# Top-k attention and a capacity-limited expert layer: all sign products on GpSimd, the pick's table in PSUM, one order for all steps

## The chip, the cores and the metric

The kernel runs on one core of a Trainium2 chip. A core has five engines with instruction queues of their own: TensorE (PE, with its weight loads as PEld), VectorE (DVE), ScalarE (ACT), GpSimd (POOL) and SyncE (SP, which issues DMAs). Each engine takes its instructions in order; where one needs what another engine makes, it waits for a semaphore. The metric is the device time of one execution in microseconds.

## The reference

Eight batches of eight heads, 576 tokens, head size 64, all float32. A score row keeps its 32 largest entries; the rest become zero after the exponential. The result is the input of a mixture of experts with eight experts, of which each keeps at most 80 tokens.

```python
scores = scale * np.matmul(q, k.transpose(0, 1, 3, 2))
kth = np.partition(scores, -top_k, axis=-1)[..., -top_k:-top_k + 1]   # top_k = 32
scores = np.where(scores >= kth, scores, -1000000000.0)
attn = np.exp(scores - np.max(scores, axis=-1, keepdims=True))
attn = attn / (np.sum(attn, axis=-1, keepdims=True) + 1e-09)
x = np.matmul(attn, v)                       # then (B, H, S, D) -> (4608, 512)

logits = x @ w_gate                          # 8 experts; the best one per token
for e in range(E):
    # the tokens of e, at most the 80 with the largest gate weight
    h = np.maximum(x[tok_idx] @ w1[e], 0.0)
    out[tok_idx] = gate_w[tok_idx, None] * (h @ w2[e])
```

## The kernel before

Attention goes over 32 head pairs (`NP`, four per batch). Of each pair, 576 query rows are cut into four full tiles of 128 rows and a tail of 64. A full tile gives two **units**, one per head; in the tail both heads share one unit of 128 rows. So a head pair has nine units (`UPP`) and the whole attention 288 (`NU`). A unit is 128 rows of 576 scores. After attention come the routing and the experts (`finish`).

What a unit goes through:

- `front`, L226 and L233: TensorE makes the scores of both heads into four PSUM banks; one ScalarE instruction copies them, scaled by a tiny power of two, to the SBUF tile `s`.
- `parts`, L241: VectorE takes the eight largest of each of six blocks of 96 columns into `cand`, six instructions.
- `search`: on the 48 candidates MAX8 (L252) and match-replace (L260) give the 24th largest, in `w9`. ScalarE's `sign` (L257) marks which scores lie below it and counts them into `cnt`. The product `y` of scores and signs (L264), for odd units on GpSimd and for even ones on VectorE, leaves the next candidates as the largest, which MAX8 (L266) finds. The **pick** (L269) compares a table `past` of nine possible counts with `cnt`, and so takes the threshold of the unit into `thr`.
- `below`, L278 and L280: the mask of all scores under the threshold, for odd units by ScalarE, for even ones by GpSimd.
- `turn_w`, L316 to L325: TensorE transposes the scores of a tile into `ab` and `cc` and adds the masks times a huge negative number (L321); two ScalarE exponentials give `wT`.
- `back`, L336: `wT` times the values, with a column of ones, into `cc`. `over`, L348: the reciprocal of the sums. `divide`, L359: two ScalarE copies per tile scale the result into the features `xn`.
- `norm`, L368 to L392: the features are stored to DRAM; transposed (`xT`, L376) and multiplied by the gate weights, they give the logits (`part` or `lg`, L388).
- `turn`, L201 and L214: transposes q and k of the next head pair; one ScalarE copy takes both out (`both`).

PSUM has eight banks here: four in the pool `ps_s`, two in `ps_w` (`ab`), two in `ps_c` (`cc`). `four()` takes a new tile of all four banks of `ps_s`, and `turn`, `front`, `norm` (twice) and the last `turn_w` use it in turn. The pool `rows` holds the big SBUF tiles.

`run` writes the order by hand (`manual_schedule`): no planner moves an instruction. In step i each letter of a string places one instruction of a unit that lies `back[c]` steps back, so that several units are in different stages. "G" is one of the six MAX8 of unit i; "a" the last of them and the first MAX8 of the search; "b", "c", "d", "e" the rest of the search of unit i-1, "e" with `sign`; "y" the product of unit i-2; "g" its MAX8 a step later; "h" the pick of unit i-4 and "m" its mask; "z" the reciprocal. After the letters a step places `turn_w` of unit i-4, the `divide`, `front` of unit i+4, `back` of unit i-5, and then `turn` or a part of `norm`.

```python
back = dict(a=0, b=1, c=1, d=1, e=1, y=2, g=3, h=4, m=4)

for c in "ghmGbGycGdGGGeaz" if i % 2 else "GbGhmgcGdGeGGyaz":
```

The weights of experts 0 to 3 load beside attention, in pieces from the list `slow` (L137), expert 4's when `finish` begins, those of 5 to 7 as buffers come free.

Of the kernel before, what the change touches and what calls it, by code (L numbers as in the profile page):

```python
# [18 lines left out]
TOP_K = 32  # L19
# [8 lines left out]
def kernel(  # L28
# [120 lines left out]
    class Attention:  # L149


        def __init__(self, stack, lean):
            self.lean = lean
            pool = lambda name, bufs, **kw: stack.enter_context(tc.tile_pool(name=name, bufs=bufs, **kw))
            self.nat, self.qkp, self.rows = pool("nat", 1), pool("qkp", 2), pool("rows", 2)
            self.small, vpool = pool("small", 4), pool("vpool", 1)
            self.ps_s, self.ps_w, self.ps_c = (pool(n, k, space=PSUM) for n, k in (("ps_s", 1), ("ps_w", 1), ("ps_c", 2)))
            self.qk, self.turned, self.lg = {}, {}, {}
            self.s, self.top, self.cnt, self.y, self.mask, self.w, self.xn = ({} for _ in range(7))
            self.thr, self.z = thr_all, z_all  # L160
# [32 lines left out]

        def four(self):
            return self.ps_s.tile([P, 4, 512], F32, name="sp", tag="sp")

# [6 lines left out]
        def turn(self, n):  # L203

            four = self.four()
            ps = [four[:, 2 * j : 2 * j + 2, :].rearrange("p j c -> p (j c)") for j in range(2)]
            both = self.qkp.tile([P, 2, S], F32, name="both", tag="both")
            self.turned[n] = both[:, 0, :], both[:, 1, :]
            for j, src in enumerate(self.qk.pop(n)):
                self.turn_in(ps[j], src.rearrange("p c h d -> p c (h d)"))  # L210
                if n == 0:
                    nc.scalar.copy(both[:, j, :], ps[j][:, :S])
            if n > 0:
                nc.scalar.copy(both, four.rearrange("p (k j) c -> p k (j c)", k=2)[:, :, :S])  # L214

        def front(self, n, t):

            qT, kT = self.turned[n]
            m = P if t < NF else TL
            i = n * UPP + 2 * t  # L220
            ps = self.four()
            for j in range(2):
                for h in range(2):
                    d = slice(D * h, D * h + D)
                    o = ps[:, 2 * h + j, :HS] if t < NF else ps[TL * h : TL * h + TL, j, :HS]
                    nc.tensor.matmul(o, lhsT=qT[d, t * P : t * P + m], rhs=kT[d, j * HS : (j + 1) * HS], start=True, stop=True)  # L226
            g = 2 if t < NF else 1
            s = self.rows.tile([P, 2 * S], F32, name="s", tag="s", bufs=2 if self.lean else 5)
            for h in range(g):
                self.s[i + h] = s[:, h * S : (h + 1) * S]  # L230
            for j in range(0, 2 * g, 2 if i == 0 else 2 * g):
                w = 2 if i == 0 else 2 * g
                nc.scalar.activation(s[:, j * HS : (j + w) * HS].rearrange("p (j c) -> p j c", c=HS), ps[:, j : j + w, :HS],  # L233
                                     Act.Copy, scale=TINY)
# [10 lines left out]
        def search(self, i):  # L245
# [4 lines left out]
            for r in range(G0 // 8):  # L250
# [8 lines left out]
                if r < G0 // 8 - 1:  # L259
                    nc.vector.match_replace(out=cand, in_to_replace=dst, in_values=cand, imm_value=LOW)  # L260
# [3 lines left out]
            engine.tensor_tensor(out=y, in0=s, in1=sign, op=Alu.mult)  # L264
            yield
            nc.vector.max(out=w9[:, 8:], in_=y)  # L266
            yield
            pick = self.small.tile([P, TOP_K - G0 + 1], F32, name="pick", tag="pick")
            nc.vector.scalar_tensor_tensor(out=pick, in0=past, scalar=cnt, in1=w9[:, 7:], accum_out=self.thr[:, i : i + 1],  # L269
                                           op0=Alu.is_equal, op1=Alu.mult)  # L270
# [11 lines left out]
        def search_all(self, i):  # L282

            s = self.s[i]
            top = self.top[i] = self.small.tile([P, TOP_K // 8, 8], F32, name="top", tag="top")
            scr = self.rows.tile([P, S], F32, name="y", tag="y", bufs=1)
            nc.vector.max(out=top[:, 0, :], in_=s)
# [12 lines left out]
        def turn_w(self, n, t):  # L300
# [3 lines left out]
            if i == NU - 1 and not self.lean:  # L304

                ab = self.four().rearrange("p h (c r) -> p h c r", r=P)
            else:
# [42 lines left out]
        def divide(self, n, t):  # L350
            if t == 0:
                self.xn[n] = self.rows.tile([P, NK, 2, D], F32, name="xn", tag="xn")
            cc = self.w.pop((n, t))
            for h in range(2):
                if t < NF:
                    p, o, j, m = slice(0, P), 2 * P + h * (D + 1), h, P
                else:
                    p, o, j, m = slice(TL * h, TL * h + TL), 2 * P, 0, TL
                nc.scalar.activation(self.xn[n][:m, t, h, :], cc[p, o : o + D], Act.Copy, scale=self.z[p, n % NP, t, j : j + 1])  # L359

        def norm(self, n, b, hp, bi, nb, cs=range(NK)):
# [9 lines left out]
            yield 1  # L371
            ps = self.four()[:, :2, :].rearrange("p j c -> p (j c)")
            at = slice(cs[0] * P, min(S, cs[-1] * P + P))
# [3 lines left out]
            yield 1  # L377
            lp = self.four()[:, 0, : NK * E].rearrange("p (c e) -> p c e", e=E)
            for c in cs:
# [48 lines left out]
        def run(self, slow):  # L428
# [17 lines left out]
            def step(i, last):  # L446
# [424 lines left out]
    with tc.If(nc.values_load(bad[0:1, 0:1]) > 0):  # L871
# [6 lines left out]
        with ExitStack() as again:  # L878
            wpool = again.enter_context(tc.tile_pool(name="wpool2", bufs=4))
            for e in range(4):  # L880
                for dma in load_w(e, wpool):
# [33 lines left out]
```

## Time and profile before

| | |
|---|---|
| median of 3 runs | 996.0 us (993.81 to 996.81) |
| profiled execution: its time / its span | 994.79 us / 993.1 us |
| VectorE busy | 870.6 us (88%), 5072 instructions |
| TensorE busy, weight loads | 885.5 us (89%), 704.9 us |
| ScalarE busy | 797.2 us (80%), 1652 instructions |
| GpSimd busy | 451.9 us (46%), 330 instructions |
| first and last pick | at 20.5 and 859.3 us |
| first expert's first matmul | at 901.2 us |

Busy time is the union of an engine's instructions. VectorE's and ScalarE's overlap by some tens of ns where they follow each other, so that the mean duration of a group is more than what one of them costs; the distance from a start to the next start, in the timeline, is the better price. A group's line gives the count, the busy time and mean duration, and after the second bar the idle time of the engine before these instructions, with who ended most of it.

### The profile page before, as it was taken

What the parts mean: (1) busy time and instruction counts of PE and PEld (TensorE: products, weight loads), DVE (VectorE), ACT (ScalarE), POOL (GpSimd) and SP (SyncE); (2) the same over time, 40 slices, a digit from 0 to 9 for tenths busy, and PEclk for the clock granted to TensorE, in tenths of its full rate; (3) what the DMA queues carried; (4) which work ended last, traced back from release to release, by engine and by line L of the source; (5) the groups of instructions that cost most, each with busy time, mean ns of one, the idle gap of its engine ahead of it and who ended that gap; (6) DMA issues with size and microseconds to landing.
All of it is one profiled execution on the core that took longest, in us unless ns stands there. A gap on an engine that the chain in (4) does not pass through costs nothing.

```text
span 993.1 us, 35590 instructions
## 1 busy us (share of the span) xinstructions
PE 885.5 (89%) x13368; PEld 704.9 (71%) x13368; DVE 870.6 (88%) x5072; ACT 797.2 (80%) x1652; POOL 451.9 (46%) x330
## 2 busy tenths in 40 slices
PE   5899999998989989899899999999899898679996
PEld 3677777776767777677677777777677676668896
DVE  5899999999999999999999999999999999571110
ACT  3899999999999989999999999999899999601110
POOL 2445555555455545554555555555455555302111
PEclk9999999999999999999999999999999999979998
DMA  3344453333332323333333322222222100044920
GB/s 72 97 126 131 129 134 92 92 92 92 91 79 62 87 82 86 92 92 93 88 82 83 91 49 51 50 50 50 50 50 49 41 23 14 16 170 142 382 76 28
DMA packets 167893, 85.76 MB, mean 86 GB/s; under 512 B 117792, under 2 KB 154656, under 8 KB 167712
## 3 DMA queue, kind: packets, MB, share of 16 engines
q1 hardware_dynamic: 166688, 80.78, 29.7%
q0 software_dynamic: 1024, 2.62, 0.9%
q8 instruction: 107, 1.75, 0.7%
q14 instruction: 74, 0.61, 0.2%
HBM read 63.19 MB, written 20.19 MB: 84 GB/s over the span
## 4 chain that ended last, share of the span: by engine, by line
DVE 53%; PE 24%; ACT 18%; issue 5%; DMA 1%; POOL 0%; POOLq 0%; SPq 0%; ACTq 0%; DVEq 0%
DVE cand L241 17%; DVE w L266 12%; DVE cand L260 6%; DVE y L264 6%; ACT s L233 4%; DVE top L252 4%; PE yp L799 4%; ACT wT L325 3%; PE sp L201 3%; PE cc L336 3%; ACT sign L257 3%; DVE pick L269 3%; ACT mask L278 2%; PE sp L226 2%; PE ab L316 2%
## 5 line engine op out<-in xcount | busy, mean ns | idle before, releaser
L241 DVE MAX8 cand<-s 128x8 f32<-128x96 f32 x1728 | 393.9, 250 | 8.9 <-ACT s L233 8.8
L280 POOL TENSOR_SCALAR mask<-s,thr_all 128x576 bf16<-128x576 f32 x144 | 248.2, 1723 | 144.9 <-DVE pick L269 121.8
L264 POOL TENSOR_TENSOR y<-s,sign 128x576 f32<-128x576 f32 x144 | 184.8, 1283 | 277.3 <-DVE pick L269 128.0
L336 PEld LDWEIGHTS cc<-vb,wT 128*64 128x64 f32 x5760 | 181.7, 138 | 111.2 <-ACT wT L325 98.5
L257 ACT ACTIVATE sign<-s,w 128x576 bf16<-128x576 f32 x288 | 225.4, 783 | 22.8 <-DVE w L252 22.2
L336 PE MATMUL cc<-vb,wT 128*64 128x65 f32 x5760 | 204.0, 225 | 40.6 <-ACT wT L325 38.9
L266 DVE MAX8 w<-y 128x8 f32<-128x576 f32 x288 | 217.8, 756 | 2.5 <-POOL y L264 2.5
L226 PE MATMUL sp<-both 64*128 64x288 f32 (+1 forms) x1280 | 202.1, 435 | 15.0 <-ACT part L388 6.5
L233 ACT ACTIVATE s<-sp 128x1152 f32<-128x1152 f32 (+1 forms) x161 | 167.3, 1040 | 12.7 <-PE sp L226 11.9
L316 PE MATMUL ab<-ident,s 128*128 128x128 f32 x1148 | 175.6, 282 | 0.0
L325 ACT ACTIVATE wT<-ab 128x1024 f32<-128x1024 f32 (+1 forms) x159 | 148.8, 936 | 0.0
L226 PEld LDWEIGHTS sp<-both 64*128 64x128 f32 (+1 forms) x1280 | 105.6, 179 | 53.8 <-ACT part L388 8.5
L316 PEld LDWEIGHTS ab<-ident,s 128*128 128x128 f32 x1148 | 127.5, 141 | 11.6 <-issue 0.9
L321 PEld LDWEIGHTS <-mask 128*128 128x128 bf16 x1440 | 92.1, 98 | 42.4 <-ACT mask L278 19.6
L252 DVE MAX8 top<-cand 128x8 f32<-128x48 f32 x576 | 116.9, 203 | 0.0
L260 DVE MATCH_REPLACE8 cand<-top,cand 128x48 f32<-128x48 f32 x576 | 112.9, 196 | 0.0
L278 ACT ACTIVATE mask<-s,thr_all 128x576 bf16<-128x576 f32 x144 | 112.3, 780 | 0.4
L264 DVE TENSOR_TENSOR y<-s,sign 128x576 f32<-128x576 f32 x144 | 107.6, 747 | 4.5 <-ACT sign L257 4.5
L359 ACT ACTIVATE xn<-cc,z_all 128x64 f32<-128x64 f32 (+1 forms) x320 | 86.5, 318 | 1.4 <-DVE z_all L348 0.8
L316 PE MATMUL cc<-ident,s 128*128 128x128 f32 x288 | 78.9, 274 | 0.3 <-ACT xn L359 0.2
L269 DVE SCALAR_TENSOR_TENSOR pick<-past,cnt,w 128x9 f32<-128x9 f32 x288 | 69.5, 241 | 0.2 <-DVE z_all L348 0.2
L323 ACT ACTIVATE wT<-cc 128x256 f32<-128x256 f32 (+1 forms) x160 | 56.2, 351 | 12.0 <-PE cc L321 11.3
(188 smaller groups left out, 965.7 us busy)
## 6 DMA issues: line engine op xcount, KB each, us to landing
w<-in_moe_w_dram SPq DMA_DIRECT2D x32, 512.0 KB, 4.7
w<-in_moe_w_dram SPq DMA_DIRECT2D x8, 2048.0 KB, 9.8
out_dram<-zero SPq DMA_DIRECT2D x9, 1024.0 KB, 6.3
qn<-in_q_dram SPq DMA_DIRECT2D x64, 128.0 KB, 2.6
kn<-in_k_dram SPq DMA_DIRECT2D x64, 128.0 KB, 2.5
vb<-in_v_dram SPq DMA_DIRECT2D x64, 128.0 KB, 2.6
xd<-xn SPq DMA_DIRECT2D x32, 256.0 KB, 4.3
qn<-in_q_dram SPq DMA_DIRECT2D x32, 32.0 KB, 2.5
```

Of the source, the lines that this page charges most:

```text
L226: nc.tensor.matmul(o, lhsT=qT[d, t * P : t * P + m], rhs=kT[d, j * HS : (j + 1) * HS], start=True, stop=True)
L233: nc.scalar.activation(s[:, j * HS : (j + w) * HS].rearrange("p (j c) -> p j c", c=HS), ps[:, j : j + w, :HS], Act.Copy, scale=TINY)
L241: nc.vector.max(out=cand[:, j, :], in_=s[:, j * S // NG : (j + 1) * S // NG])
L252: nc.vector.max(out=dst, in_=cand)
L257: nc.scalar.activation(sign, s, Act.Sign, bias=w9[:, 7:8], scale=-1.0, accum_out=cnt)
L260: nc.vector.match_replace(out=cand, in_to_replace=dst, in_values=cand, imm_value=LOW)
L264: engine.tensor_tensor(out=y, in0=s, in1=sign, op=Alu.mult)
L266: nc.vector.max(out=w9[:, 8:], in_=y)
L280: nc.gpsimd.tensor_scalar(self.mask[i], self.s[i], self.thr[:, i : i + 1], None, op0=Alu.is_lt)
L316: nc.tensor.matmul(dst[h][c], lhsT=sc[:, keys[c]], rhs=ident, start=c == 0 or (c == NF and h == 0), stop=False, is_transpose=True, skip_gr ...
L325: nc.scalar.activation(wT[:, : g * NF, :], ab.rearrange("p h c r -> p (h c) r")[:, : g * NF, :], Act.Exp, scale=scale / TINY)
L336: nc.tensor.matmul(cc[r : r + TL, o], lhsT=wT[:, h * NF + c if c < NF else 2 * NF + h, r : r + TL], rhs=vb[:, c, h if t < NF else r // TL, ...
```

## The change

All 288 products go to GpSimd, and the tile `y` gets two buffers. The features of a full tile are made by one VectorE product out of PSUM, with the reciprocals spread over the columns; the tail's by two. The tile `banks` takes the four PSUM banks once and for all; `four(w, step)` gives views of it, and its last 16 columns hold a copy of the table `past`, which the pick now reads. One string gives the order of all steps, with the pick first and the features ("x") last. To make room for the second `y`, the weight pool has three buffers and the late one two: expert 3's weights load in `finish`.

```diff
-            self.ps_s, self.ps_w, self.ps_c = (pool(n, k, space=PSUM) for n, k in (("ps_s", 1), ("ps_w", 1), ("ps_c", 2)))
+            ps_s, self.ps_w, self.ps_c = (pool(n, k, space=PSUM) for n, k in (("ps_s", 1), ("ps_w", 1), ("ps_c", 2)))
+            self.banks = ps_s.tile([P, 4 * 512], F32, name="banks")
+            self.past = self.banks[:, 4 * 512 - 16 :][:, : TOP_K - G0 + 1]
+            nc.vector.tensor_copy(self.past, past)
...
-        def four(self):
-            return self.ps_s.tile([P, 4, 512], F32, name="sp", tag="sp")
+        def four(self, w, step=512):
+            t = self.banks[:, :]
+            return bass.AP(t.tensor, t.offset, [list(t.ap[0]), [step, 4 * 512 // step], [1, w]])
...
-            y = self.rows.tile([P, S], F32, name="y", tag="y", bufs=1)
-            engine = nc.gpsimd if i in self.odd else nc.vector
-            engine.tensor_tensor(out=y, in0=s, in1=sign, op=Alu.mult)
+            y = self.rows.tile([P, S], F32, name="y", tag="y")
+            nc.gpsimd.tensor_tensor(out=y, in0=s, in1=sign, op=Alu.mult)
...
-            nc.vector.scalar_tensor_tensor(out=pick, in0=past, scalar=cnt, in1=w9[:, 7:], accum_out=self.thr[:, i : i + 1],
+            nc.vector.scalar_tensor_tensor(out=pick, in0=self.past, scalar=cnt, in1=w9[:, 7:], accum_out=self.thr[:, i : i + 1],
...
+            o, xn, z = 2 * P, self.xn[n], self.z[:, n % NP, t, :].unsqueeze(2)
+            if t < NF:
+                nc.vector.tensor_tensor(out=xn[:, t, :, :], in0=cc[:, o : o + 2 * (D + 1)].rearrange("p (h d) -> p h d", h=2)[:, :, :D],
+                                        in1=z.to_broadcast([P, 2, D]), op=Alu.mult)
+                return
             for h in range(2):
...
-                nc.scalar.activation(self.xn[n][:m, t, h, :], cc[p, o : o + D], Act.Copy, scale=self.z[p, n % NP, t, j : j + 1])
+                p = slice(TL * h, TL * h + TL)
+                nc.vector.tensor_tensor(out=xn[:TL, t, h, :], in0=cc[p, o : o + D], in1=z[p, 0, :].to_broadcast([TL, D]), op=Alu.mult)
...
-                for c in "ghmGbGycGdGGGeaz" if i % 2 else "GbGhmgcGdGeGGyaz":
+                for c in "hmybGcGdGeGGGgzax":
...
+                    elif c == "x":
+                        for u in drawn:
+                            self.divide(*u)
...
-                for u in done:
-                    self.divide(*u)
...
-        late = stack.enter_context(tc.tile_pool(name="late", bufs=1))
-        for dma in load_w(4, late):
-            dma()
+        late = stack.enter_context(tc.tile_pool(name="late", bufs=2))
+        for e in (3, 4):
+            for dma in load_w(e, late):
+                dma()
...
-        wpool = main.enter_context(tc.tile_pool(name="wpool", bufs=4))
-        for e in range(4):
+        wpool = main.enter_context(tc.tile_pool(name="wpool", bufs=3))
+        for e in range(3):
             slow += load_w(e, wpool, 4)
```

More of the change, by code (lines that the diff above doesn't have):

```diff
@@ L203, in turn @@
         def turn(self, n):
-            four = self.four()
-            ps = [four[:, 2 * j : 2 * j + 2, :].rearrange("p j c -> p (j c)") for j in range(2)]
+            ps = self.four(S, 1024)
             both = self.qkp.tile([P, 2, S], F32, name="both", tag="both")
@@ L209, in turn @@
             for j, src in enumerate(self.qk.pop(n)):
-                self.turn_in(ps[j], src.rearrange("p c h d -> p c (h d)"))
+                self.turn_in(ps[:, j, :], src.rearrange("p c h d -> p c (h d)"))
                 if n == 0:
-                    nc.scalar.copy(both[:, j, :], ps[j][:, :S])
+                    nc.scalar.copy(both[:, j, :], ps[:, j, :])
             if n > 0:
-                nc.scalar.copy(both, four.rearrange("p (k j) c -> p k (j c)", k=2)[:, :, :S])
+                nc.scalar.copy(both, ps)
         def front(self, n, t):
@@ L220, in front @@
             i = n * UPP + 2 * t
-            ps = self.four()
+            ps = self.four(HS)
             for j in range(2):
@@ L224, in front @@
                     d = slice(D * h, D * h + D)
-                    o = ps[:, 2 * h + j, :HS] if t < NF else ps[TL * h : TL * h + TL, j, :HS]
+                    o = ps[:, 2 * h + j, :] if t < NF else ps[TL * h : TL * h + TL, j, :]
                     nc.tensor.matmul(o, lhsT=qT[d, t * P : t * P + m], rhs=kT[d, j * HS : (j + 1) * HS], start=True, stop=True)
@@ L232, in front @@
                 w = 2 if i == 0 else 2 * g
-                nc.scalar.activation(s[:, j * HS : (j + w) * HS].rearrange("p (j c) -> p j c", c=HS), ps[:, j : j + w, :HS],
+                nc.scalar.activation(s[:, j * HS : (j + w) * HS].rearrange("p (j c) -> p j c", c=HS), ps[:, j : j + w, :],
                                      Act.Copy, scale=TINY)
@@ L285, in search_all @@
             top = self.top[i] = self.small.tile([P, TOP_K // 8, 8], F32, name="top", tag="top")
-            scr = self.rows.tile([P, S], F32, name="y", tag="y", bufs=1)
+            scr = self.rows.tile([P, S], F32, name="y", tag="y")
             nc.vector.max(out=top[:, 0, :], in_=s)
@@ L304, in turn_w @@
             if i == NU - 1 and not self.lean:
-                ab = self.four().rearrange("p h (c r) -> p h c r", r=P)
+                ab = self.four(1024, 2048).rearrange("p o (h c r) -> p (o h) c r", h=2, r=P)
             else:
@@ L353, in divide @@
             cc = self.w.pop((n, t))
-            for h in range(2):
[L355 to L359, printed above, removed]
+            o, xn, z = 2 * P, self.xn[n], self.z[:, n % NP, t, :].unsqueeze(2)
[3 more added lines that the diff above has]
+                return
+            for h in range(2):
+                p = slice(TL * h, TL * h + TL)
+                nc.vector.tensor_tensor(out=xn[:TL, t, h, :], in0=cc[p, o : o + D], in1=z[p, 0, :].to_broadcast([TL, D]), op=Alu.mult)
         def norm(self, n, b, hp, bi, nb, cs=range(NK)):
@@ L371, in norm @@
             yield 1
-            ps = self.four()[:, :2, :].rearrange("p j c -> p (j c)")
+            ps = self.four(1024, 2048)[:, 0, :]
             at = slice(cs[0] * P, min(S, cs[-1] * P + P))
@@ L377, in norm @@
             yield 1
-            lp = self.four()[:, 0, : NK * E].rearrange("p (c e) -> p c e", e=E)
+            lp = self.four(NK * E, 2048)[:, 0, :].rearrange("p (c e) -> p c e", e=E)
             for c in cs:
@@ L878 @@
         with ExitStack() as again:
-            wpool = again.enter_context(tc.tile_pool(name="wpool2", bufs=4))
-            for e in range(4):
+            wpool = again.enter_context(tc.tile_pool(name="wpool2", bufs=3))
+            for e in range(3):
                 for dma in load_w(e, wpool):
```

## The prediction

> **What bounds the kernel now.** I read the page's engine table first, then the table by stage, the groups, and last one stretch of the timeline. The stage table's row for 450 to 550 us shows what the attention loop looks like all the way from 50 to 850 us:
>
> ```profile
> 450.00:550.00 100.00, 90.35 (x1303) 70.69 (x1302) 99.44 (x592) 92.45 (x191) 51.11 (x34) 1.00 0.35 90
> ```
>
> The columns are length, then busy time of PE, PEld, DVE, ACT, POOL, then clock, DMA share, GB/s. VectorE is busy 99.44 of 100 us; ScalarE (92.45) and TensorE (90.35) are close behind; GpSimd has half its time free. The groups say what VectorE does, and what the change touches:
>
> ```profile
> L266 DVE MAX8 w<-y 128x8 f32<-128x576 f32 x288 | 217.8, 756 | 2.5 <-POOL y L264 2.5
> L264 POOL TENSOR_TENSOR y<-s,sign 128x576 f32<-128x576 f32 x144 | 184.8, 1283 | 277.3 <-DVE pick L269 128.0
> L264 DVE TENSOR_TENSOR y<-s,sign 128x576 f32<-128x576 f32 x144 | 107.6, 747 | 4.5 <-ACT sign L257 4.5
> L359 ACT ACTIVATE xn<-cc,z_all 128x64 f32<-128x64 f32 (+1 forms) x320 | 86.5, 318 | 1.4 <-DVE z_all L348 0.8
> ```
>
> Half of the products take 747 ns on VectorE, half 1283 ns on GpSimd. The picks' first and last start (20.5 and 859.3 us, from their line's own answer) give 838.8 / 287 x 9 = 26.3 us for a head pair's nine units. Of the timeline I need one step, because what counts is the distance from one start to the next, and who starts after whom:
>
> ```profile
> 507.05 0.21 DVE L269 SCALAR_TENSOR_TENSOR pick<-past,cnt,w 128x9 f32<-128x9 f32 x1
> 507.19 0.26 DVE L241 MAX8 cand<-s 128x8 f32<-128x96 f32 x1
> 507.36 0.07 DVE L260 MATCH_VALUE_LOAD cand<-top,cand 128x8 f32 x1
> 507.53 0.25 DVE L241 MAX8 cand<-s 128x8 f32<-128x96 f32 x1
> 507.69 0.19 DVE L252 MAX8 top<-cand 128x8 f32<-128x48 f32 x1
> 507.80 0.24 DVE L241 MAX8 cand<-s 128x8 f32<-128x96 f32 x1
> ...
> 508.57 0.23 PE L321 MATMUL cc<-huge,mask 128*128 128x128 bf16 x1 [0.33 <-ACT mask L278]
> 508.62 0.19 DVE L252 MAX8 w<-cand 128x8 f32<-128x48 f32 x1
> 508.64 0.39 PE L321 MATMUL ab<-huge,mask 128*128 128x128 bf16 x4
> ...
> 508.90 0.78 ACT L257 ACTIVATE sign<-s,w 128x576 bf16<-128x576 f32 x1 [0.39 <-DVE w L252]
> 508.96 1.24 PE L226 MATMUL sp<-both 64*128 64x288 f32 x8
> 509.43 0.21 DVE L269 SCALAR_TENSOR_TENSOR pick<-past,cnt,w 128x9 f32<-128x9 f32 x1
> 509.68 0.36 ACT L323 ACTIVATE wT<-cc 128x256 f32<-128x256 f32 x1
> 509.82 1.72 POOL L280 TENSOR_SCALAR mask<-s,thr_all 128x576 bf16<-128x576 f32 x1 [0.60 <-DVE pick L269]
> 509.94 1.01 ACT L325 ACTIVATE wT<-ab 128x1024 f32<-128x1024 f32 x1
> ...
> 511.24 1.15 ACT L233 ACTIVATE s<-sp 128x1152 f32<-128x1152 f32 x1
> ```
>
> Start to start: pick 0.14, MAX8 of 96 and match-replace 0.17 each, MAX8 of 48 0.11; the chain of waits adds MAX8 of 576 0.67, product 0.66, reciprocal 0.07.
>
> [...] the picks' median is 214 ns, their longest 1286 ns, as long as one GpSimd product (1283). [...]
>
> **The change, part by part.**
>
> *Products.* 144 of 0.66 us leave VectorE: -95 us of its time. GpSimd then has per two units 2 x 1.28 + 1.72 = 4.3 us, below the 5.84 us that two units take now; with the buffer `y` doubled its result has a step to arrive in. It costs nothing as long as two units take over 4.3 us.
>
> *Features.* 320 ScalarE copies go (86.5 us busy, beside VectorE's work). VectorE gets 128 products of 128 columns and 64 of 64. No such row exists; between L392's 40 columns (0.10 us from start to start) and L264's 576 (0.66) a line gives 0.19 and 0.12. Bounds: 0.10 (no slower than 40 columns) and 0.30 (PSUM as an input costing half again). Taken: 128 x 0.19 + 64 x 0.12 = 32 us (20 to 58).
>
> *Pick's table.* The blocked picks are worth little: 288 x (0.158 mean - 0.136 median spacing) = 6 us. Reading the table from PSUM is not in the trace as a cost: the reciprocal, which reads PSUM, has 0.07 us from start to start, so -0.02 to +0.05 a pick, taken as 0. So VectorE's own work per head pair is 9 x 2.45 (pick 0.14, two match-replaces 0.34, six MAX8 of 96 0.97, three of 48 0.33, MAX8 of 576 0.67) + 5 x 0.07 + 4 x 0.19 + 2 x 0.12 + 0.1 = 23.5 us.
>
> *The wait that the table brings.* `past` now lies in the last 16 columns of the tile `banks`, which every user of `four()` shares. In the built program's list of instructions with their semaphores, no pick of before waits for ScalarE; in the changed one 249 of 288 do, each for the last ScalarE instruction that read `banks` in the step before: 156 for the score copy (L233 before), 31 each for `both` (L214), `xT` (L376) and `part` (L388). These are reads against reads. And `front`'s first matmul waits for the step's pick. VectorE runs in order, so all of the step (six MAX8, the search, the next reductions) queues behind a pick that stands first in the new order "hmybGcGdGeGGGgzax".
>
> That closes a loop. In a step where `turn_w` runs, pick(i-4) gives a mask, TensorE adds it, then scores the next tile; ScalarE does sign(i-1), the two exponentials, then the score copy; the next step's pick waits for that copy. From the pick's start:
>
> - w9 starts at 0.14 + 0.17 + 0.16 + 0.11 + 0.16 + 0.17 + 0.16 = 1.07; sign 0.28 later (508.62 to 508.90) at 1.35; first exponential 0.78 later at 2.13; second +0.26 at 2.39; the copy +0.91 (second exponential to the next ScalarE start, 509.94 to 510.85) at 3.30; +1.15 and 0.03 to VectorE: **4.48**. The other leg is ready earlier: ScalarE's mask ends near 1.1, TensorE's five matmuls near 1.6, the scores (1.24) near 2.8.
> - Where the second mask is GpSimd's (every other head pair, as 9 is odd): mask at 0.39 (509.43 to 509.82), +1.72 = 2.11, +0.05 to TensorE, +0.46 (508.57 to 509.03), +0.04 to ScalarE = 2.66, then +0.26, +0.91, +1.15, +0.03: **5.01**.
>
> Against VectorE's own 2.45 to 2.71 such a step stalls by about 2 us, four times per head pair. The other five steps: one with no copy to wait for, 2.48; `xT`: 2.13 + 0.64 + 0.03 = 2.80; `both`: 2.13 + 1.13 + 0.03 = 3.29 (TensorE's ten transposes end near 2.0); the tail's scores: 2.13 + 0.65 + 0.03 = 2.81; the tail's exponentials and `part`: 3.75 behind GpSimd's mask, 3.1 behind ScalarE's. Sums: 4 x 4.48 + 2.48 + 2.80 + 3.29 + 2.81 + 3.75 = 33.05, and 4 x 5.01 + 2.48 + 2.80 + 3.29 + 2.81 + 3.1 = 34.5; mean 33.8 us against 26.3. Score copies with a waiting pick are 156 of 160, 31.2 head pairs' worth: +7.5 x 31.2 = +234 us. The VectorE time saved is inside this sum; so is the cover for every edit costed at nothing.
>
> *Weights.* Expert 3 no longer loads beside attention (8 DMAs of 512 KB leave SP's slow list) but in `finish`, ahead of expert 4: two more DMAs of 2 MB on SP's queue. Expert 4's 4 MB land in about 12 us from 869.3 (332 to 383 GB/s there); 8 MB would take some 24, to 893. Expert 3 starts 25.4 us after expert 0 (901.2 to 926.6), the first gather comes near 896. Nothing waits: 0 (up to 5, should the gathers meet the second load). The 133.8 us from the last pick to the end stay.
>
> Sum: 994.8 (the profiled execution, span 993.1) + 234 = 1229; the median of the runs shown, 996.0, lies 1.2 above it: 1230.
>
> **Rivals.**
> - *The waits are met when VectorE gets there.* For it: VectorE is the bound, and copies are short. Then its 23.5 us decide, with TensorE next (0.904 x 26.3 = 23.8) and some coupling, 24.5 us: 996 - 1.8 x 31.2 = 940. Against: the copy would have to end within 2.7 us of the step's pick, while mask, TensorE, exponentials and copy alone, without sign, take over 4. This is the rival on the other side; it decides if the copy of a step ends before that step's last MAX8 of 48.
> - *Half the loop.* If ScalarE's legs overlap more than the starts above allow (sign and the exponentials out of the way, steps near 3.6), a head pair takes some 30: 996 + 3.7 x 31.2 = 1110.
> - *GpSimd becomes the bound.* Its products would have to stretch from 1.28 to over 2.06 us (2 x 2.06 + 1.72 = 5.84) before this alone reaches the time before; about 1000. In the trace they range from 1273 to 1297 ns beside a busy VectorE.
> - *The table frees nothing and hurts nothing*: that is the first rival without its 6 us, 946.
>
> **How the numbers follow.** The loop as summed: 0.88; half of it 0.07; waits met (with or without the 6 us) 0.03; GpSimd 0.02. An error of 0.3 us in each long step is 0.3 x 125 = 38 us, and as much again over the five others at half the size; so 1230 carries about -70 and +60, and the range is 1160 to 1290. 0.3% of 996, 3 us, is about what a measurement of this kernel can tell from no change. Faster 0.03, same 0.01, slower 0.96.
>
> **What would show it.** Right: the pick has the largest idle time on VectorE, released by the score copy, some 2 us x 125; VectorE's busy share falls to about 0.65 to 0.7 of an attention stretch, and ScalarE's and TensorE's with it; GpSimd's products keep 1.28 us; a head pair takes 33 to 35 us; picks longer than 0.3 us are gone. Wrong: picks with no idle time before them, or VectorE at 95% and more.

## The result, and the profile after

The changed kernel takes 1263.1 us in the median (1257.3 to 1266.9, four runs) beside 994.9 us for the kernel before on the same chip: a ratio of 1.2688, with an interval of 1.2629 to 1.2747. It is slower, as forecast, by 268 us instead of 234: the forecast of 1230 us was 33 us short. The profiled execution took 1266.9 us, its span is 1265.2 us.

The stage table's row for 450 to 550 us, of the changed kernel (length, busy PE, PEld, DVE, ACT, POOL, clock, DMA share, GB/s):

```profile
450.00:550.00 100.00, 74.89 (x985) 56.74 (x983) 70.66 (x447) 67.15 (x117) 54.62 (x39) 0.93 0.23 62
```

VectorE was busy 99.44 us of these 100 and is now busy 70.66. TensorE and ScalarE fell with it, so none of the engines is the bound. Read the last figures too: TensorE's granted clock, 1.00 before, is 0.93. The prediction has no term for that.

The groups of the pick, the product and the MAX8 behind it (busy and mean of one, then the idle time of the engine just before them, and who ended most of it):

```profile
L268 POOL TENSOR_TENSOR y<-s,sign 128x576 f32<-128x576 f32 x288 | 362.0, 1278 | 14.4 <-ACT sign L262 14.4
L273 DVE SCALAR_TENSOR_TENSOR pick<-banks,cnt,w 128x9 f32<-128x9 f32 x288 | 65.5, 228 | 307.3 <-ACT s L238 239.5
L270 DVE MAX8 w<-y 128x8 f32<-128x576 f32 x288 | 214.0, 743 | 0.9 <-POOL y L268 0.9
```

GpSimd does all 288 products at the old 1278 ns each, and the MAX8 that needs them finds them ready (0.9 us of idle time in the whole run). VectorE stands still before the pick instead: 307.3 us. The view of all waits, cut to those of the picks (total, times, longest), says for what:

```profile
DVE pick L273 <- ACT s L238: 239.5, 131, 3.3
DVE pick L273 <- ACT both L219: 34.0, 31, 6.9
DVE pick L273 <- ACT part L394: 17.8, 21, 1.0
DVE pick L273 <- ACT xT L382: 10.5, 28, 1.5
```

The pick needs nothing that these four instructions make; they read the tile `banks`, in whose last columns the table lies. The score copy of a full tile and `both` read all four banks, the table's among them. `part` reads 40 columns of the first bank and `xT` at most 576 of the first two, while the table lies in the fourth; yet in all 21 waits for `part` the pick starts 0.03 us after that copy ends. So the waits in this program go by more than the table's bank. 239.5 us in 131 waits are 1.83 us each; the prediction said "some 2 us x 125".

One long step in the timeline, from a pick to the next, with ScalarE's mask (start, duration, instruction; idle time before it and who ended it, in brackets):

```profile
600.40 0.23 DVE L273 SCALAR_TENSOR_TENSOR pick<-banks,cnt,w 128x9 f32<-128x9 f32 x1 [0.27 <-ACT xT L382]
600.66 0.78 ACT L282 ACTIVATE mask<-s,thr_all 128x576 bf16<-128x576 f32 x1 [0.30 <-DVE pick L273]
...
601.51 0.19 DVE L257 MAX8 w<-cand 128x8 f32<-128x48 f32 x1
...
601.79 0.78 ACT L262 ACTIVATE sign<-s,w 128x576 bf16<-128x576 f32 x1 [0.35 <-DVE w L257]
...
602.57 0.36 ACT L327 ACTIVATE wT<-cc 128x256 f32<-128x256 f32 x1
...
602.83 1.01 ACT L329 ACTIVATE wT<-ab 128x1024 f32<-128x1024 f32 x1
602.94 0.29 DVE L360 TENSOR_TENSOR xn<-cc,z_all 128x128 f32<-128x128 f32 x1
603.73 1.13 ACT L238 ACTIVATE s<-banks 128x1152 f32<-128x1152 f32 x1
...
604.89 0.23 DVE L273 SCALAR_TENSOR_TENSOR pick<-banks,cnt,w 128x9 f32<-128x9 f32 x1 [1.66 <-ACT s L238]
```

VectorE's last work of the step, the feature product, starts at 602.94. Then it waits 1.66 us while ScalarE ends the exponentials and copies the scores; 0.03 us after that copy the next pick starts. From pick to pick 4.49 us.

Over the run, from one head pair's first pick to the next one's, the mean is 34.73 us instead of 26.40. That accounts for the profiled difference of 1266.9 - 994.8 = 272 us: 31 head pairs x 8.33 = 258; the last one +1; the first pick, at 26.6 instead of 20.5 us because it waits 6.86 us for `both`, +6; from the last pick to the end 140.5 instead of 133.6 us, +7.

### The profile page after: what moved, and what is told of

The parts are those of the page before. It is cut to its first block, busy times and chain, and to the rows that moved or that the text cites. A ratio compares the mean times of both kernels' runs of the same rounds, so it can differ in the third digit from the quotient of the medians.

```text
span 1265.2 us, 35233 instructions
## 1 busy us (share of the span) xinstructions
PE 963.4 (76%) x13368; PEld 751.9 (59%) x13368; DVE 836.8 (66%) x5121; ACT 769.0 (61%) x1332; POOL 623.9 (49%) x474
## 4 chain that ended last, share of the span: by engine, by line
DVE 30%; ACT 27%; PE 26%; POOL 11%; issue 6%; DMA 0%; ACTq 0%; POOLq 0%; SPq 0%
ACT s L238 11%; POOL mask L284 10%; DVE cand L246 10%; PE banks L231 9%; ACT sign L262 8%; DVE cand L265 5%; DVE pick L273 5%; DVE w L270 3%; PE yp L806 3%; PE cc L340 3%; ACT both L219 3%; DVE top L257 2%; ACT wT L329 2%; DVE w L257 2%; PE banks L207 2%
## 5 line engine op out<-in xcount | busy, mean ns | idle before, releaser
L246 DVE MAX8 cand<-s 128x8 f32<-128x96 f32 x1728 | 376.3, 246 | 8.5 <-ACT s L238 8.5
L268 POOL TENSOR_TENSOR y<-s,sign 128x576 f32<-128x576 f32 x288 | 362.0, 1278 | 14.4 <-ACT sign L262 14.4
L340 PEld LDWEIGHTS cc<-vb,wT 128*64 128x64 f32 x5760 | 213.8, 158 | 133.6 <-ACT wT L329 111.0
L340 PE MATMUL cc<-vb,wT 128*64 128x65 f32 x5760 | 237.1, 246 | 52.5 <-ACT wT L329 52.3
L273 DVE SCALAR_TENSOR_TENSOR pick<-banks,cnt,w 128x9 f32<-128x9 f32 x288 | 65.5, 228 | 307.3 <-ACT s L238 239.5
L231 PE MATMUL banks<-both 64*128 64x288 f32 (+1 forms) x1280 | 227.2, 479 | 26.5 <-DVE pick L273 22.0
L238 ACT ACTIVATE s<-banks 128x1152 f32<-128x1152 f32 (+1 forms) x161 | 165.0, 1026 | 39.3 <-PE banks L231 34.5
L231 PEld LDWEIGHTS banks<-both 64*128 64x128 f32 (+1 forms) x1280 | 114.4, 193 | 69.7 <-DVE pick L273 23.5
L325 PE MATMUL cc<-minus,mask 128*128 128x128 bf16 x144 | 32.8, 228 | 139.7 <-POOL mask L284 139.2
L325 PE MATMUL cc<-huge,mask 128*128 128x128 bf16 x144 | 32.3, 224 | 49.5 <-ACT mask L282 49.5
```

What stands on the lines that cost most here:

```text
L246: nc.vector.max(out=cand[:, j, :], in_=s[:, j * S // NG : (j + 1) * S // NG])
L268: nc.gpsimd.tensor_tensor(out=y, in0=s, in1=sign, op=Alu.mult)
L340: nc.tensor.matmul(cc[r : r + TL, o], lhsT=wT[:, h * NF + c if c < NF else 2 * NF + h, r : r + TL], rhs=vb[:, c, h if t < NF else r // TL, ...
```

## The experiments

Two theories: **the loop**, as in the prediction (a pick bound to the banks that ScalarE reads costs most of it), and **the other parts** (products, features, order or weights cost it, and the pick's wait only shows the time that they take). The kernels first move the table alone, then look into the missing 33 us, then put the table elsewhere, and at last make each other part by itself.

**The changed kernel with the pick's table back in SBUF.** All else stays.

```diff
-            nc.vector.scalar_tensor_tensor(out=pick, in0=self.past, scalar=cnt, ...
+            nc.vector.scalar_tensor_tensor(out=pick, in0=past, scalar=cnt, ...
```

> The changed kernel with one operand put back: the pick reads the table past in SBUF again, and no pick waits for a reader of the four banks. Theory (the picks' waits for ScalarE's reads of the banks close the loop): the loop is gone, VectorE's own 23.5 us per head pair and TensorE's 23.8 decide, 24 to 25 us per head pair, 925 to 960 us; up to 15 us more if picks block on GpSimd's products, which now run twice as often. Rival (products on GpSimd, or the pick as the first letter of the step, cost the time): 1230 to 1265 us, as the changed kernel. Rival (features on VectorE): above 1200 us.

Measured: 1033.7 us, ratio 1.0386 (1.0367 to 1.0406). The 229 us that go are the loop's, for nothing else was changed. But the gain that should have appeared beneath it is not there: the time lies above the expected 925 to 975 us. The pick's line (count, then min, median and max of one in ns), and its group:

```profile
L273 DVE SCALAR_TENSOR_TENSOR pick<-past,cnt,w x288: 168/231/1291, 19.7 to 893.4; 128x9 f32<-128x9 f32 x144
L273 DVE SCALAR_TENSOR_TENSOR pick<-past,cnt,w 128x9 f32<-128x9 f32 x288 | 141.8, 492 | 0.7 <-DVE top L257 0.3
```

The mean is 492 ns, the longest 1291; 135 of 288 picks take over 300 ns, where 17 did before. Over 214 ns each, they cost 80 us, and VectorE counts them as busy: no wait shows it. The kernel before has the same in small: its 17 picks over 300 ns (459 to 1286) each ran beside a GpSimd product and ended 24 to 28 ns after it, and no pick that started during a product was shorter. Now there are twice as many GpSimd products. With the table in PSUM, in the changed kernel, 82 picks overlap a product, and none takes over 231 ns. The "6 us" that the prediction gives to blocked picks held roughly for the kernel before (8 by this measure); with all products on GpSimd the same item is 80 us. Taking the table out of SBUF had a reason; the place that it was given was the trouble.

**The kernel before with only the table moved into `banks`.** Products, order, features and weights stay as they were.

```diff
+            self.banks = ps_s.tile([P, 4 * 512], F32, name="banks")
+            self.past = self.banks[:, 4 * 512 - 16 :][:, : TOP_K - G0 + 1]
...
-            nc.vector.scalar_tensor_tensor(out=pick, in0=past, scalar=cnt, ...
+            nc.vector.scalar_tensor_tensor(out=pick, in0=self.past, scalar=cnt, ...
```

> The kernel before with one part of the change alone: the shared tile of four banks with the table in its last columns, and the pick reading it there; products half and half, two order strings, features by ScalarE as before. Theory: the loop closes here too, and is longer, as ScalarE's feature copies (0.4 us) stand ahead of the score copy and the sign comes later after the pick; 5.2 to 5.5 us in the four long steps of a head pair and 2.9 in the short ones, 34 to 37 us per head pair, 1230 to 1340 us. Rival (order or products are the cause): 990 to 1005 us.

Measured: 1411.3 us, ratio 1.4185 (1.414 to 1.423), 39.4 us a head pair: more than the range expected, and worse than the whole change. Alone, the table costs 416 us. The waits of VectorE name the same release:

```profile
DVE pick L273 <- ACT s L237: 339.8, 155, 3.2
```

ScalarE's feature copies and the old order are still in the loop there; its long steps have medians of 5.2 to 6.1 us, at a clock of 0.877 (94 windows of 3.41 us at half rate in attention, against 43 in the changed kernel; how much of the excess is theirs was not separated). The loop theory stands: the table is enough to cause the loss, and the other parts together make it smaller.

**The clock: filling TensorE's wait.** The loop's sum missed some 24 us of head pairs. In the changed kernel's trace the clock is not 0.93 throughout: between the first and the last pick it is 0.50 in 43 windows of 3.41 us, two of them in a row, and 1.00 elsewhere. The kernel before has one such window there, at 851 us, just ahead of its last pick. The stage table around one of them, and around one of the more usual kind:

```profile
625.55:628.96 3.41, 0.14 (x3) 0.00 (x0) 3.38 (x21) 1.41 (x3) 1.60 (x1) 1.00 0.00 0
628.96:632.37 3.41, 3.23 (x19) 2.00 (x21) 2.63 (x7) 1.83 (x5) 2.60 (x3) 0.50 0.01 2
632.37:635.78 3.41, 3.29 (x59) 2.91 (x56) 2.41 (x16) 2.92 (x6) 0.00 (x0) 1.00 0.01 2
...
714.29:717.70 3.41, 1.46 (x17) 1.09 (x17) 2.83 (x18) 1.87 (x5) 2.89 (x2) 1.00 0.56 127
717.70:721.11 3.41, 3.41 (x47) 2.54 (x44) 1.24 (x12) 2.36 (x3) 1.31 (x2) 0.50 0.03 5
```

In the first window TensorE worked 0.14 us; in the next it has half its clock. In the lower pair it worked 1.46 us, and the clock fell as well. The timeline of the step around the first, one with GpSimd's mask:

```profile
626.96 0.22 DVE L273 SCALAR_TENSOR_TENSOR pick<-banks,cnt,w 128x9 f32<-128x9 f32 x1
...
627.36 1.72 POOL L284 TENSOR_SCALAR mask<-s,thr_all 128x576 bf16<-128x576 f32 x1 [3.77 <-DVE pick L273]
...
629.14 0.29 PE L325 MATMUL cc<-minus,mask 128*128 128x128 bf16 x1 [3.45 <-POOL mask L284]
...
629.78 2.29 PE L231 MATMUL banks<-both 64*128 64x288 f32 x8
...
632.20 1.13 ACT L238 ACTIVATE s<-banks 128x1152 f32<-128x1152 f32 x1 [1.29 <-PE banks L231]
...
633.37 0.23 DVE L273 SCALAR_TENSOR_TENSOR pick<-banks,cnt,w 128x9 f32<-128x9 f32 x1 [1.71 <-ACT s L238]
```

TensorE idles 3.45 us for the mask; the eight score matmuls then take 2.29 us, not the 1.24 us of the kernel before, and now it is they for whom the copy waits. The step lasts 6.41 us instead of 5.0; it is one of the three longest of its kind, whose median is 5.80. The windows at half rate are 3.41 us long in this trace and start whole multiples of it apart (489.01 and 506.08 are 5 apart). In the window ahead of the 42 stretches at half rate TensorE had worked 0.12 to 2.26 us, 1.46 in the median, and every window of attention with under 1.75 us was followed by half rate. The edit puts 24 small matmuls of zeros, which add nothing, before the second mask where that is GpSimd's:

```diff
+                if h == 1 and i + h not in self.odd and not self.lean:
+                    for _ in range(FILL):      # FILL = 24
+                        nc.tensor.matmul(dst[0][0], lhsT=zero.bitcast(BF16)[:, :P], rhs=zero.bitcast(BF16)[:, :P], start=False, ...
```

> The changed kernel, with 24 matmuls of zeros (128x128, bf16) that add nothing to the scores put between the two halves of the masks wherever the second mask is GpSimd's, so that TensorE isn't idle while it waits there. Theory (the 30 us by which the changed kernel is over the sum of its steps come from the clock of TensorE, 0.93 here and 1.00 before, lowered after its idle stretches): clock above 0.98, the two long steps of odd head pairs that take 5.8 and 5.4 us come down to 5.0 to 5.1, and the time falls by 15 to 35 us, to 1228 to 1248. Rival (those steps are long for another reason, GpSimd's queue or VectorE's order): the time stays at 1255 to 1268, or rises by the matmuls' own 1.4 us x 64 = 90 us where TensorE is the limit.

Measured: 1253.7 us, ratio 1.2611 (1.259 to 1.2632), 9 us less than the changed kernel and between the two expectations, with every run under the changed kernel's fastest (1256.5 against 1257.3 us); clock 0.971, and 15 windows at half rate instead of 43. Head pairs without GpSimd's second mask do not move (mean 33.20 to 33.19 us), those with it go from 36.37 to 35.47: 15 x 0.90 = 13 us of the spans' 14. More TensorE work made the kernel faster and raised the granted clock from 0.932 to 0.971, so the clock is part of the miss. The size was expected too large, for two reasons that the trace shows: the fill lengthens one step by 0.26 us (5.03 to 5.29), and 15 windows stay.

**The table in a bank of `cc`.** Same change, but the table lies in the last 16 columns of the two `cc` tiles, which become persistent and alternate; a pick reads the one that the coming `turn_w` takes next.

```diff
+            self.cc = [self.ps_c.tile([P, 512], F32, name=f"cc{j}") for j in range(2)]
+            self.past = [t[:, 512 - 16 :][:, : TOP_K - G0 + 1] for t in self.cc]
...
-            nc.vector.scalar_tensor_tensor(out=pick, in0=self.past, scalar=cnt, ...
+            nc.vector.scalar_tensor_tensor(out=pick, in0=self.past[self.tiles % 2], scalar=cnt, ...
...
-            cc = self.ps_c.tile([P, 512], F32, name="cc", tag="cc")
+            cc = self.cc[self.tiles % 2]
+            self.tiles += 1
```

> The changed kernel with the table moved, still in PSUM, from the tile of four banks to the last columns of the two cc banks, which are now kept for good and used in turn; the pick reads the table in the cc bank that the next turn_w will take, which no other engine is about to use. In the built program no pick waits for a copy out of the four banks. Theory (the bank shared with ScalarE's copies is the whole loss, and PSUM takes away the 80 us of picks that wait for GpSimd's products in e1_sbuf_table): 1034 - 80 = 954, less the stalls that these picks pass on, 930 to 965 us; picks of 0.23 us, 24 to 25 us per head pair. Rival (the order or GpSimd's products hold the step up beside the picks): 1000 to 1035 us.

Measured: 988.9 us, ratio 0.992 (0.9903 to 0.9936). The loop is gone, 274 us with it; the result lies between the two expectations. Most steps take 2.54 and 2.75 us, where the prediction's own-work sum had 2.45 and 2.71, and one wait is left, at the first pick of a head pair:

```profile
DVE pick L276 <- PE cc L344: 32.7, 28, 2.1
```

Since the tail has one unit and not two, `back` of the last full tile is then still writing that `cc`: once more a shared tile, here a single bank, and not a value.

**The same with the features by ScalarE's copies again**, at the letter "x".

```diff
-                nc.vector.tensor_tensor(out=xn[:, t, :, :], in0=cc[:, o : o + 2 * (D + 1)]..., in1=z.to_broadcast([P, 2, D]), op=Alu.mult)
+                nc.scalar.activation(self.xn[n][:m, t, h, :], cc[p, o : o + D], Act.Copy, scale=self.z[p, n % NP, t, j : j + 1])
```

> f1_cc_table with the features made by ScalarE's two copies per tile as before (at the letter x), so that it differs in them alone. Theory: VectorE saves 32 us of products, ScalarE gets 86 us of copies and is at 24 us of work per head pair, ahead of the score copy on its queue; ScalarE then decides: 0 to 30 us more than f1_cc_table. Rival (the features' move is what costs or frees nothing): equal to f1_cc_table within 5 us; if VectorE alone decides, 15 to 30 us less than it.

Measured: 1047.1 us, ratio 1.0516 (1.0498 to 1.0533), 58 us more than with VectorE's products: outside the expectation.

```profile
DVE pick L276 <- ACT xn L367: 119.1, 138, 2.1
```

The copies read `cc`, so ScalarE holds the table's bank again. With the features on VectorE, what was left to wait for were the matmuls of `back`. So this placement and the move of the features belong together; neither could be judged alone.

**The first pick of each head pair reads SBUF**, the other eight `cc`.

```diff
-                in0=self.past[self.tiles % 2]
+                in0=past if i % UPP == 0 else self.past[self.tiles % 2]
```

> f1_cc_table, but the first unit of each head pair (32 of 288) takes the table from SBUF: in f1_cc_table its pick waits 0.9 to 1.4 us for back's matmuls in the cc bank that it reads. Theory ([...] the SBUF copy at worst waits for one GpSimd product): the step before that pick falls from 3.97 and 3.39 us to 2.6 to 3.2, 10 to 35 us less than f1_cc_table, 955 to 980 us. Rival (TensorE is by now the limit behind that wait): within 5 us of f1_cc_table, 985 to 990.

Measured: 966.1 us, ratio 0.9705 (0.9687 to 0.9724), as expected. Picks are no longer among the waits. Half of the moved picks still pay, though: 16 of the 32 that read SBUF take 0.85 to 1.28 us, as busy time, some 10 us in all, while no pick that reads `cc` takes over 0.23 us. The stage row is that of a VectorE-bound loop again, at full clock:

```profile
450.00:550.00 100.00, 92.41 (x1343) 73.12 (x1338) 99.61 (x615) 86.49 (x159) 73.01 (x52) 1.00 0.19 45
```

**The small sums of the routing on GpSimd.** Other VectorE operations with two SBUF inputs run long in the trace of the table in `cc`: the sum of the logits lasts up to 0.97 us (0.20 at best for its 40 columns), the product `R` up to 1.32 us (0.16). The expectation's 1.23 and 1.29 us from start to start hold over 1 us of idle time behind the operation each. In the changed kernel 28 operations of the routing run long, 322 to 1315 ns, and each ends 45 to 101 ns after a GpSimd product. 37 instructions move.

```diff
-                nc.vector.tensor_tensor(out=lg, in0=lg, in1=part, op=Alu.add)
+                nc.gpsimd.tensor_tensor(out=lg, in0=lg, in1=part, op=Alu.add)
...
-                nc.vector.tensor_tensor(out=r4, in0=o4, in1=s4, op=Alu.mult)
+                nc.gpsimd.tensor_tensor(out=r4, in0=o4, in1=s4, op=Alu.mult)
```

> f3_first_sbuf with two more two-input VectorE operations on GpSimd: the sum of the logits (25) and the routing products R (12). In f1_cc_table they last up to 1.23 and 1.29 us from start to start, where the shortest are 0.20 and 0.09: they wait for GpSimd's products. Theory [...]: 25 x 0.3 + 12 x 0.5 = 13 us less, and what the steps behind pass on, 5 to 25 us less than f3_first_sbuf. Rival (their time is their own): 0 to 5 us.

Measured: 956.8 us, ratio 0.962 (0.9603 to 0.9637). This is the fastest version: 38 us under the kernel before, 306 under the changed one. The 9 us that went fit what the two had lost over their unblocked durations in the kernel with the first pick in SBUF, 8.7 us.

**Half of the products back on VectorE**, in the kernel with the first pick in SBUF; the letter "y" moves to the end of the step, where VectorE can do a product without waiting for `sign`.

```diff
-            nc.gpsimd.tensor_tensor(out=y, in0=s, in1=sign, op=Alu.mult)
+            engine = nc.gpsimd if i in self.odd else nc.vector
+            engine.tensor_tensor(out=y, in0=s, in1=sign, op=Alu.mult)
...
-                for c in "hmybGcGdGeGGGgzax":
+                for c in "hmbGcGdGeGGGygzax":
```

> f3_first_sbuf with the even units' products back on VectorE, and the letter y moved behind the step's MAX8 so that the sign is there in time: it differs in where 144 products run. Theory (VectorE is the bound once no pick waits): 144 x 0.66 = 95 us more on VectorE, of which 60 to 95 show, 1020 to 1070 us; GpSimd busy 0.45 of the attention in place of 0.73. Rival (GpSimd's products hold VectorE up as much as they free it): within 20 us of f3_first_sbuf.

Measured: 1045.8 us, ratio 1.0511 (1.0485 to 1.0536). Where the table is out of the way, moving the products is worth 80 us in this order. With the same split of products as the kernel before, this one is 50 us slower than it; the features' products, some 40 us on VectorE, are the largest part of that.

**Each other part alone in the kernel before.** First the weights of expert 3 in `finish`:

```diff
-        late = stack.enter_context(tc.tile_pool(name="late", bufs=1))
-        for dma in load_w(4, late):
-            dma()
+        late = stack.enter_context(tc.tile_pool(name="late", bufs=2))
+        for e in (3, 4):
+            for dma in load_w(e, late):
+                dma()
...
-        for e in range(4):
+        for e in range(3):
             slow += load_w(e, wpool, 4)
```

> The kernel before with expert 3's weights moved into `finish`, nothing else. Prediction's term: 0, up to +5 us, after the last pick. From the stretches after the last pick in the other kernels (133.6 us before, 134.9 with the table alone, 137.9 to 141.7 with the weights moved): +3 to +8 us, all of it after the last pick; attention unchanged at 26.3 us a head pair. Rival: those differences came from the rest of the change; then 994 to 996 us.

Measured: 997.1 us over ten runs, ratio 1.0028 (1.0016 to 1.0039): +2.8 us, just under the 3 to 8 expected. The trace has the last pick no later (858.2 against 859.3 us), and 135.6 us from it to the end.

Then the features by VectorE's products:

```diff
-                nc.scalar.activation(self.xn[n][:m, t, h, :], cc[p, o : o + D], Act.Copy, scale=self.z[p, n % NP, t, j : j + 1])
+                nc.vector.tensor_tensor(out=xn[:, t, :, :], in0=cc[:, o : o + 2 * (D + 1)]..., in1=z.to_broadcast([P, 2, D]), op=Alu.mult)
```

> The kernel before with the features made by VectorE's products out of PSUM, at the place where ScalarE's copies stood, nothing else. VectorE is the bound (99.44 of 100 us) and gets 128 x 0.21 + 64 x 0.2 = 40 us at the spacing measured in the changed kernel: +25 to +40 us. Rival: ScalarE, which loses 86 us of copies, was holding VectorE up in places, and gives part of it back: +0 to +20 us. Second rival: the product waits for nothing of its own here, but the products of GpSimd lock it out: over +40.

Measured: 1050.5 us, ratio 1.0551 (1.0533 to 1.0569), +56 us: over the expectation, but not by blocking (3 picks over 300 ns, 17 before). The timeline shows the price:

```profile
480.96 0.17 DVE L348 RECIPROCAL z_all<-cc 128x2 f32<-128x2 f32 x1
481.16 0.29 DVE L356 TENSOR_TENSOR xn<-cc,z_all 128x128 f32<-128x128 f32 x1
481.37 0.25 DVE L241 MAX8 cand<-s 128x8 f32<-128x96 f32 x1
```

The product needs the reciprocal just ahead of it: 0.187 us from start to start in the median, where 0.068 is usual with other work between. That is 160 x 0.12 = 19 us, beside 128 x 0.208 + 64 x 0.243 = 42 us for the products; 6 us come back from picks no longer blocked. 19 + 42 - 6 = 55. The step to another kind of instruction is not what costs: in the changed kernel the same product starts 0.12 us after a MAX8 of 48 that it does not need. The new order string, with "a" between "z" and "x", hides the 19.

Then the products, all on GpSimd, in the old order, with the weights moved to make room for the second `y`:

```diff
-            y = self.rows.tile([P, S], F32, name="y", tag="y", bufs=1)
-            engine = nc.gpsimd if i in self.odd else nc.vector
+            y = self.rows.tile([P, S], F32, name="y", tag="y")
+            engine = nc.gpsimd
```

> The kernel before with all products on GpSimd, two buffers for `y` and expert 3's weights in `finish` (room for the second `y`); table in SBUF, old order, ScalarE's copies. VectorE loses 144 x 0.66 = 95 us; if that were all, TensorE (0.904 x 26.3 = 23.8 us a head pair) would leave about 925 to 940 us. My theory: twice as many products of GpSimd lock twice as many of the picks, which read two SBUF inputs (80 us over the unlocked picks in the changed kernel with its table in SBUF): 960 to 1000 us, with 100 picks or more over 300 ns.

Measured: 1159.6 us, ratio 1.165 (1.1633 to 1.1668); missed. The blocked picks are there, 126 of them, 70 us over 214 ns. The larger item is a wait that had not been thought of:

```profile
DVE w L266 <- POOL y L264: 147.3, 124, 1.8
```

In the old order an even step has "y" near its end, and the next step begins with "g", its MAX8. What VectorE did in place is now a product of 1.28 us on GpSimd, and VectorE waits 1.19 us for it each time. With 95 us of products gone from VectorE these two leave some 122 of the 165 us; the rest lies in other small operations, the sums of the logits above all (16 us more than before).

Last, the new order with two `y` and the weights moved, but products and table as before:

```diff
-                for c in "ghmGbGycGdGGGeaz" if i % 2 else "GbGhmgcGdGeGGyaz":
+                for c in "hmybGcGdGeGGGgzax":
```

> The kernel before with the one order of letters for all steps, the two buffers of y that it needs, and the weight pools of three and two; products half on VectorE, features by ScalarE (issued at the letter x), table in SBUF. Theory: VectorE has the work of before, 26 us per head pair, and no new wait: 985 to 1010 us. Rival (the order with the pick first makes the step long): above 1150 us. The second load in the last part costs under 5 us by either.

Measured: 1134.7 us, ratio 1.1398 (1.1377 to 1.1418); missed. The opposite wait:

```profile
DVE y L264 <- ACT sign L257: 120.2, 106, 3.6
```

With "y" early in the step, VectorE's own products stand in line before ScalarE has made the sign. So the order and the products' move need each other: +140 and +165 us apart, a gain together once the table is out of the way.

## Why the prediction was right, point by point

- **The loop.** Right, in kind and in its legs. The step shown above has w9 at 1.11 us after the pick (1.07 predicted), sign 1.39 (1.35), the exponentials at 2.17 and 2.43 (2.13, 2.39), the copy at 3.33 (3.30), the next pick at 4.49 (4.48). The waits for `xT` and `part` come about as predicted, too (28 and 21 of them), though those two do not read the table's bank. With GpSimd's mask, steps without a slow window last 5.03 us (5.01).
- **The other five steps.** Medians of 2.48, 2.82 and 3.30 against 2.48, 2.80 and 3.29; the tail's scores 2.83 (2.81), its exponentials 3.52 and 3.03 (3.75, 3.1). The sum for pairs whose second masks are ScalarE's, 33.05, was measured as 33.20.
- **Where the 33 us went missing: the sum of the other kind of pair, 34.5.** It was measured as 36.37, as it took TensorE's five matmuls and its scores at the durations of before. Two long steps of such pairs mostly meet half the clock: medians 5.80 and 5.38 instead of 5.03. (36.37 - 34.5) x 15 = 28 us. Filling TensorE's wait took back 13 of them; that all of the rest is the clock too was not shown. The wait itself follows from the prediction's own legs: a mask that comes 2.1 us after the pick, and a step that had already stalled. What it left out is that TensorE's idle time had a price of its own here: 43 windows of 3.41 us at a clock of 0.50. The range up to 1290 held the result by a margin that was reckoned for errors of 0.3 us in the long steps, not for the clock; that it was wide enough is in part luck.
- **Start and end.** The first pick's wait, 6 us, was not in the sum. "Weights: 0 (up to 5)" was 2.8 us. The other 4 us after the last pick are not settled; the features' products alone, with no weights moved, have 137.2 us there instead of 133.7, in one trace each.
- **Features.** 0.208 us for 128 columns (0.19 taken, 0.10 to 0.30; that an input from PSUM might cost half again was the author's guess), but 0.229 and 0.256 for the tail's two of 64 (0.12): 42 us, not 32, inside the stall here and so without effect on the forecast. A straight line through the number of columns was wrong for the small ones.
- **Pick's table.** Its input from PSUM costs 0.15 us from start to start against 0.136: within the bounds. No pick over 300 ns is left, as said (the longest takes 231).
- **GpSimd** kept its 1.28 us, and VectorE's busy share, 0.71, came out just above the 0.65 to 0.7 given.
- **The rival "waits met", 940 us,** did not come true, and as a sum for the change without its wait it was somewhat low: with the table elsewhere, 988.9, then 966.1 and 956.8 us. Missing in it: small VectorE operations blocked behind GpSimd's products (moving 37 of them was worth 9 us), the first picks (23 us), and steps of 2.53 and 2.75 us. Products off VectorE brought 80 us, not 95.

## What to carry to other kernels

A small constant in a shared PSUM tile made its reader wait here for copies out of that tile, 307 us over the run, and in a bank of `cc` still 33 us for matmuls. So place such a constant by who uses the tile when it is read, not by where 16 columns are free: the place decided between 1263 and 989 us, and 957 with what was left of waits and blocks thinned out. Of the 307 us, 237 were behind score copies of full tiles, which read the table's own bank. If an in-order engine waits at the start of each step for the end of another engine's step, sum the legs of that loop from start-to-start times, and look at which engines now idle: TensorE paid a second time here for windows in which it worked under 1.75 of 3.41 us. Parts that look independent can need each other; a part tried alone in the old order tells its price there, not its worth in the change.

## What the runs showed of the hardware

- A VectorE operation on nine columns with two SBUF inputs, the pick, took up to 1291 ns where GpSimd made all products at 1280 ns each, in 135 of 288 cases over 300 ns; with its table in PSUM, in the changed kernel, none of 288 did (231 at most). It counted as busy time: the view of waits has 0.7 us before these picks.
- TensorE's clock was at half for 3.41 us after windows in which it had worked 0.12 to 2.26 of 3.41 us, 1.46 in the median of 42 cases. In the changed kernel every window with under 1.75 us was followed by one at half rate. Small matmuls of zeros in the gap cut such windows from 43 to 15.
- A VectorE instruction that reads what the one just before it wrote started 0.187 us after it in the median (a reciprocal of two columns and the product of features, in the kernel before with the features on VectorE); the next instruction starts 0.068 us after that reciprocal where it does not need it.
